# Two MLPs behind LSH attention on one core: order of tasks with a shared port, first norm on VectorE, 45 split tiles on GpSimd

## The chip, the cores and the metric

The kernel runs on one core of one Trainium2 chip. The metric is the device time of one execution in microseconds (us). Five engines work side by side, each in the fixed order of its own instructions: TensorE (PE; its weight loads are listed as PEld), VectorE (DVE), ScalarE (ACT), GpSimd (POOL) and SyncE (SP), which issues the DMAs.

## The reference

```python
batch, n_heads, seq, head_dim = (2, 8, 768, 64)      # attention, 6 hash bits
mask = q_bucket[:, :, :, None] == k_bucket[:, :, None, :]
scores = scale * np.matmul(q, k.transpose(0, 1, 3, 2))
scores = np.where(mask, scores, -1000000000.0)
attn = softmax(scores); x = attn @ v                 # then 1536 tokens x 512
...
xn = x / rms * rms_g                                  # first MLP, d_ff 1536
x = (silu(xn @ w_gate) * (xn @ w_val)) @ w_out
...
h = x @ w_in                                          # second MLP, d_ff 2048
out = elu(h) @ w2_out
```

All values are float32, the weights arrive as float64.

## The kernel before

Every product is made from operands split into a rounded high part and a low rest, so each matmul of the MLPs runs three times (high by high, high by rest, rest by high). The split costs vector work: ScalarE writes the high part, VectorE or GpSimd subtracts it from the value to get the rest.

The attention goes in eight pairs of heads, numbered 0 to 7 here. For a pair, GpSimd writes each head's q and k twice side by side (`twice`, tile `rd`), TensorE transposes it (`prep_T`, `ps_t`), ScalarE and VectorE split it into the operands `tq` and `tk`, and GpSimd copies two of the parts (`tq<-tq`, `tk<-tq`). Hash bits (`ps_b`) and bucket marks (`ps_c`) follow. A pair has six units, each of two blocks of 128 queries: `score` (`ps_s`, the maximum `nm` on VectorE, the exponential on ScalarE), `turn` (three transposed tiles `ps_p` of 128x512 for each unit, each split into `pt`) and `weigh` (`ps_v`). The split of a unit's first tile is done by GpSimd where the table `BYPOOL` names the unit (`phi`, `plo`, from a copy `pf` that ScalarE makes), and by VectorE (L531) elsewhere. `post` divides by the sums of the exponentials (`r`), and `norm` makes the RMS norm of a batch once its four pairs are done: behind pair 3 for the first batch, behind pair 7 for the second. The first norm runs on GpSimd (`newton`, `scale2`, `lo`), the second on VectorE (`scale`).

The weights come in ten groups of matrix parts. `weights` loads a part, ScalarE and VectorE turn its float64 words into float32 (`c1` to `c5`, tile `wf`, L808 to L831), ScalarE writes the high part and GpSimd the rest `wlo` (L856). The first group may be loaded once pair 5 has begun. Then come the MLPs: `hidden` (`ps_h`), `reduce1` (`ps_y`) and `reduce2` (`ps_o`, added to `oa` and stored).

Nothing of this is issued in the order of the text. `Plan` collects tasks with an engine, a duration, what they read and write, and a priority; `Plan.order` then takes, again and again, the task that can start first by these planned durations, and of several the one of lowest priority number. That sequence is each engine's program. The priorities are shifted by the table `OFF`, some 100 numbers. PSUM has four single banks (`bank`) and two double ones (`bank2`); SBUF buffers come from pools of 24 slots, 9 halves and 4 `pt` tiles.

The opening sets constants: on VectorE `wtmp` and `ctmp` (L1085 to L1097) and the projection `pj` (L1114 to L1120), on GpSimd the identity and the fields `bitt` (L1104, L1105).

Of the kernel before, what the change touches and what calls it, by code (L numbers as in the profile page):

```python
# [24 lines left out]
POOL_COPY = 0.82  # L25
# [6 lines left out]
OFF = {'S': [-0.384, -0.596, -1.82, 16.69, -0.785, -0.843, -0.281, -0.374], 'max': [107.091, 86.229, 74.287, 78.306, 4.65, 29.877, -1.002, 35.125], 'exp': [62.941, 112.551, 91.27, 19.546, 123.248, 62.234, 18.002, -5.545], 'T': [0.813, 0.913, 0.365, 0.876, 0.651, 1.113, 1.459, 0.993], 'hi': [19.733, -62.022, -7.959, -72.894, 51.659, 4.387, -74.284, -78.51], 'lo': [37.269, 76.285, 5.085, -95.768, -79.38, 8.342, -31.826, -0.586], 'V': [2.187, 1.975, 1.986, 1.909, 1.876, 2.208, 2.458, 2.096], 'my': [-17.276, -32.546, -64.73, -54.909, -121.029, -34.033, -7.347, -44.516], 'ld': [46.975, -7.846, 214.522, -35.192, 37.247, 221.876, -5.026, -66.279], 'pv': [56.573, -26.315, 46.952, -98.676, 75.721, 70.124, -94.292, -41.006], 'prep': [-0.879, -2.624, -3.589, -0.3, -0.223, -0.105, 0.276, -67.519], 'post': [5.051, 5.005, 2.459, 1.85, 3.722, 8.338, 2.173, 8.692], 'plo': [-134.549, 11.751, -83.073, -44.746, 0.084, -16.015, 72.021, -31.41], 'wc': -3.034, 'ld1': 96.489, 'norm0': -2.712, 'rush': 35.741, 'pstep': 0.316, 'qstep': 0.017, 'norm': 31.762, 'w0': 122.867, 'w0s': 1023313562453027.6}  # L32


class Plan:
# [10 lines left out]
    def __init__(self, caps):  # L46
        self.caps = caps
        self.tasks = []
        self.last_w, self.readers, self.touch, self.duty = {}, {}, {}, {}

    def add(self, eng, us, fn, r=(), w=(), prio=None, lat=0.0, tab=None, duty=1.0):
# [21 lines left out]
        self.duty[i] = duty  # L73
        return i

    def order(self):
# [11 lines left out]
        clock = {}  # L88
        table = None
# [14 lines left out]
        while len(out) < n:  # L104
            best = None
            for eng, lst in ready.items():
                now = clock[eng]
                fits = []
                for i in lst:
                    _, us, fn, deps, bufs, prio, lat, tab = self.tasks[i]  # L110
                    t = max(now, at[i])
                    need = {}
# [42 lines left out]
            clock[eng] = t + us  # L155
            end[i] = t + us + lat
# [22 lines left out]
def kernel(  # L179
# [117 lines left out]
    def prep_v(j, prio):  # L297
# [14 lines left out]
        for a in range(2):  # L312
            plan.add("Pool", 1.4, lambda a=a: hi(a), [("h3", "vn", j)], [(("slot", "vv", j), a, 0)], prio)
# [943 lines left out]
```

## Time and profile before

| | |
|---|---|
| three runs | 861.0, 860.9, 860.76 us, median 860.9 |
| profiled execution | 861.95 us, of which the span of the instructions is 860.2 |
| granted TensorE clock | 0.995 of full speed |
| busy share | PE 97%, DVE 75%, ACT 51%, POOL 32% |
| the chain that ended last | PE 80%, DVE 12%, ACT 4%, POOL 3% of the span |

A share is an average over stages. Pair 0's first score stands at 19.9 us of the span, pair 4's at 142.2, pair 5's at 178.5, pair 6's at 221.8; the last score and the first matmul of the MLPs lie at 280 to 282, and the second batch's norm begins at 309. "Idle" of an engine is time without an instruction in the profile's rows; TensorE's matmuls overlap, and their ends are modelled.

### The profile page before, as it was taken

What the parts mean: (1) busy time and instruction counts of PE and PEld (TensorE: products, weight loads), DVE (VectorE), ACT (ScalarE), POOL (GpSimd) and SP (SyncE); (2) the same over time, 40 slices, a digit from 0 to 9 for tenths busy, and PEclk for the clock granted to TensorE, in tenths of its full rate; (3) what the DMA queues carried; (4) which work ended last, traced back from release to release, by engine and by line L of the source; (5) the groups of instructions that cost most, each with busy time, mean ns of one, the idle gap of its engine ahead of it and who ended that gap; (6) DMA issues with size and microseconds to landing.
All of it is one profiled execution on the core that took longest, in us unless ns stands there. A gap on an engine that the chain in (4) does not pass through costs nothing.

```text
span 860.2 us, 12464 instructions
## 1 busy us (share of the span) xinstructions
PE 836.1 (97%) x4722; PEld 738.2 (86%) x4722; DVE 648.7 (75%) x1020; ACT 440.7 (51%) x831; POOL 279.2 (32%) x295
## 2 busy tenths in 40 slices
PE   7999999998999899999999999999999999999998
PEld 6899999887899799989889898887888888888786
DVE  8999899999999999443265555678856878677754
ACT  3889888898888655332222322245544333332321
POOL 8766576699745322110011110210201111111100
PEclk9999999999999999999999999999999999999999
DMA  5102012240002201211111312204221302001003
GB/s 165 39 19 64 12 38 75 60 146 35 19 2 75 74 1 38 85 31 44 49 50 50 98 50 99 74 1 146 74 74 37 110 25 74 25 25 50 1 12 135
DMA packets 25708, 49.05 MB, mean 57 GB/s; under 512 B 2480, under 2 KB 8880, under 8 KB 25648
## 3 DMA queue, kind: packets, MB, share of 16 engines
q1 hardware_dynamic: 25648, 48.25, 17.2%
q8 instruction: 37, 0.61, 0.3%
q14 instruction: 23, 0.19, 0.1%
HBM read 45.09 MB, written 3.15 MB: 56 GB/s over the span
## 4 chain that ended last, share of the span: by engine, by line
PE 80%; DVE 12%; ACT 4%; POOL 3%; issue 1%; POOLq 0%; DVEq 0%; ACTq 0%
PE ps_h L905 36%; PE ps_o L1044 14%; PE ps_y L990 11%; PE ps_s L474 5%; PE ps_v L566 5%; PE ps_p L519 5%; DVE pt L531 2%; PE ps_t L347 2%; DVE nm L481 2%; PE ps_b L395 1%; ACT p L491 1%; DVE wf L817 1%; DVE wf L824 1%; DVE wf L831 1%; ACT pt L527 1%
## 5 line engine op out<-in xcount | busy, mean ns | idle before, releaser
L856 POOL TENSOR_TENSOR wlo<-wf,whi 128x768 fp32r<-128x768 f32 (+1 forms) x54 | 87.4, 1618 | 444.8 <-ACT whi L852 430.5
L905 PE MATMUL ps_h<-xn,whi 128*128 128x512 f32 (+2 forms) x768 | 190.1, 336 | 2.9 <-DVE pt L531 1.1
L905 PEld LDWEIGHTS ps_h<-xn,whi 128*128 128x128 f32 x768 | 133.6, 189 | 15.6 <-DVE pt L531 1.4
L905 PE MATMUL ps_h<-xn,wlo 128*128 128x256 f32 (+2 forms) x384 | 128.9, 336 | 0.0
L1044 PE MATMUL ps_o<-whi,h 128*128 128x512 f32 (+1 forms) x388 | 118.9, 388 | 0.7 <-DVE oa L1056 0.6
L905 PE MATMUL ps_h<-y,whi 128*128 128x512 f32 x384 | 118.2, 389 | 0.0
L930 ACT ACTIVATE sg<-ps_h 128x512 f32<-128x512 f32 (+1 forms) x87 | 50.6, 583 | 112.6 <-PE ps_h L905 110.4
L852 ACT CAST whi<-wf 128x768 fp32r<-128x768 f32 (+1 forms) x54 | 39.6, 734 | 125.1 <-DVE wf L831 125.0
L566 PE MATMUL ps_v<-pt,vv 128*128 128x256 f32 x576 | 97.9, 296 | 2.2 <-DVE tk L358 1.0
L951 ACT CAST h<-hf 128x512 fp32r<-128x512 f32 (+1 forms) x87 | 51.7, 605 | 88.7 <-DVE hf L936 47.0
L481 DVE TENSOR_REDUCE nm<-ps_s 128x1 f32<-128x768 f32 x96 | 90.8, 946 | 3.1 <-PE ps_s L474 2.4
L990 PE MATMUL ps_y<-h,whi 128*128 128x512 f32 (+1 forms) x312 | 91.3, 373 | 1.3 <-DVE ya L1002 1.3
L491 ACT ACTIVATE p<-ps_s,nm 128x768 f32<-128x768 f32 x96 | 87.2, 909 | 8.3 <-DVE nm L481 7.6
L519 PE MATMUL ps_p<-ident,p 128*128 128x128 f32 x576 | 87.5, 278 | 3.4 <-DVE pt L531 2.6
L474 PE MATMUL ps_s<-tk,tq 128*128 128x384 f32 x384 | 88.2, 351 | 1.0 <-ACT p L491 0.9
L955 DVE TENSOR_TENSOR h<-hf,h 128x512 fp32r<-128x512 f32 (+1 forms) x87 | 69.5, 812 | 25.9 <-ACT h L951 25.1
L1044 PEld LDWEIGHTS ps_o<-whi,h 128*128 128x128 f32 x388 | 72.1, 188 | 16.7 <-DVE oa L1056 2.2
L905 PEld LDWEIGHTS ps_h<-y,whi 128*128 128x128 f32 x384 | 72.1, 188 | 15.0
L936 DVE TENSOR_TENSOR hf<-ps_h,sg 128x512 f32<-128x512 f32 (+1 forms) x39 | 25.2, 647 | 79.0 <-PE ps_h L905 79.0
L566 PEld LDWEIGHTS ps_v<-pt,vv 128*128 128x128 f32 x576 | 78.7, 189 | 5.4 <-DVE pt L531 1.9
L531 DVE TENSOR_TENSOR pt<-ps_p,pt 128x512 fp32r<-128x512 f32 x120 | 80.6, 681 | 3.6 <-ACT pt L527 2.2
L519 PEld LDWEIGHTS ps_p<-ident,p 128*128 128x128 f32 x576 | 67.3, 142 | 12.3 <-DVE pt L531 4.6
(109 smaller groups left out, 1521.3 us busy)
## 6 DMA issues: line engine op xcount, KB each, us to landing
wraw<-in_moe_w_out_dram SPq DMA_DIRECT2D x12, 768.0 KB, 5.1
wraw<-in_moe_w_in_dram SPq DMA_DIRECT2D x8, 768.0 KB, 4.7
wraw<-in_moe_w_out_dram SPq DMA_DIRECT2D x10, 512.0 KB, 4.0
raw<-in_q_dram SPq DMA_DIRECT2D x16, 192.0 KB, 3.1
raw<-in_k_dram SPq DMA_DIRECT2D x16, 192.0 KB, 3.5
vn<-in_v_dram SPq DMA_DIRECT2D x8, 384.0 KB, 3.2
wraw<-in_moe_w_gate_dram SPq DMA_DIRECT2D x4, 768.0 KB, 4.8
wraw<-in_moe_w_val_dram SPq DMA_DIRECT2D x4, 768.0 KB, 4.5
```

Source lines behind the costliest of these rows:

```text
L474: nc.tensor.matmul(st[B_][:, hf, 0:HS], lhsT=tq[:, x, c * 128:(c + 1) * 128], rhs=tk[:, x, hf * HS:(hf + 1) * HS], start=(x == 0), stop=(x ...
L481: nc.vector.tensor_reduce(out=st["nm", u, cc], in_=st[B_][:, :, 0:HS], axis=AX.XY, op=ALU.max, negate=True,)
L491: nc.scalar.activation(out=halves(st["p", u][:, cc]), in_=st.pop(B_)[:, :, 0:HS], func=AF.Exp, bias=st["nm", u, cc], scale=1.0, accum_out= ...
L519: nc.tensor.transpose(out=st[B_][:, o:o + 128], in_=p[:, cc, (2 * n + kt) * 128:(2 * n + kt + 1) * 128], identity=ident,)
L531: nc.vector.tensor_tensor(out=pt[:, 1], in0=st.pop(B_), in1=f(pt[:, 0]), op=ALU.subtract)
L566: nc.tensor.matmul(st[B_][:, 0:256], lhsT=st["vv", j][:, a, 2 * n + kt, :], rhs=pt[:, x, kt * 256:(kt + 1) * 256], start=(n == seq[0] and ...
L856: nc.gpsimd.tensor_tensor(out=l, in0=s["w"], in1=f(h), op=ALU.subtract)
L905: nc.tensor.matmul(ps[:, o:o + ln], lhsT=w[wp][:, kk, ft * 128:(ft + 1) * 128], rhs=t[xp][:, s:s + ln], start=(kk == 0 and n == 0), stop=( ...
L951: nc.scalar.copy(out=st["h", g, blk, ft][:, 0, 0:bw], in_=s["hf"])
L955: nc.vector.tensor_tensor(out=h[:, 1, 0:bw], in0=s["hf"], in1=f(h[:, 0, 0:bw]), op=ALU.subtract)
L990: nc.tensor.matmul(s["ps"][:, 0:bw], lhsT=wo[wp][:, ft, m * 128:(m + 1) * 128], rhs=h[:, xp, 0:bw], start=(ft == 0 and i == 0), stop=(ft = ...
L1044: nc.tensor.matmul(s["ps"], lhsT=h[:, xp, t * 128:(t + 1) * 128], rhs=wo[wp][:, ft, ds], start=(ft == 0 and i == 0), stop=(ft == n - 1 and ...
```

## The change

The planner gets a flag for each task that uses the port which VectorE and GpSimd share: all GpSimd tasks, and those of VectorE that work on SBUF alone. A flagged task is planned to start no sooner than the last flagged one ended. The first norm moves to VectorE, with the code that the second one uses (on ScalarE it issues a load of the activation table ahead of it). GpSimd splits 45 first tiles of units in place of 24: pair by pair 6, 6, 6, 6, 6, 6, 6, 3 in place of 5, 4, 6, 2, 2, 2, 2, 1. `wlo` is written in two halves (twice as many instructions of half the size). In the opening, two of the first four copies `rd` go to VectorE and one to ScalarE, `ctmp` takes three instructions in place of nine, and `bitt` is set by ScalarE. Of the last three sums one uses a single bank. All numbers of `OFF` differ, so the order does everywhere. The names `same_half` and `under` stand for `again` and `across`; their ScalarE forms are not selected.

```diff
-BYPOOL = ([0, 1, 2, 3, 4], [0, 2, 3, 4], [0, 1, 2, 3, 4, 5], [2, 4], [2, 4], [2, 4], [2, 4], [0])
+BYPOOL = ([0, 1, 2, 3, 4, 5], [0, 1, 2, 3, 4, 5], [0, 1, 2, 3, 4, 5], [0, 1, 2, 3, 4, 5], [0, 1, 2, 3, 4, 5], [0, 1, 2, 3, 4, 5], [0, 1, 2, 3, 4, 5], [0, 1, 5])
+FIRST = ('DVE', 'DVE', 'Pool', 'ACT')
+NORM = ('DVE', 'DVE')
...
+        self.port[i] = port or eng == "Pool"
...
+                    if self.port[i]:
+                        t = max(t, port)
...
+            if self.port[i]:
+                port = t + us
...
     def twice(j, a, i, prio):
+        eng = FIRST[2 * a + i] if j == 0 else "Pool"
...
+            cp = {"Pool": nc.gpsimd.tensor_copy, "DVE": nc.vector.tensor_copy, "ACT": nc.scalar.copy}[eng]
...
-        plan.add("Pool", pool(cols), lo, [W_, (H_, part)], [(L_, part)], prio)
+        for x in range(2):
+            plan.add("Pool", pool(cols // 2), lambda x=x: lo(x), [W_, (H_, part)], [(L_, part, x)], prio)
...
+        spare = groups[g][4] and tt >= B * S // 128 - 2 and (tt + ds.start // wd) % 2
+        B_ = ("bank" if spare else "bank2", "o", g, tt, ds.start)
...
-        nc.vector.memset(c[:, 1, 0], 0.0)
-        for i in range(NB):
-            t = ones_of(c[:, 1, 0], i)
-            nc.vector.tensor_scalar(out=t, in0=t, scalar1=-1.0, scalar2=None, op0=ALU.add)
-        nc.vector.tensor_copy(out=c[:, 1, 1], in_=c[:, 1, 0])
-        nc.vector.tensor_scalar(out=c[:, 0], in0=c[:, 1], scalar1=1.0, scalar2=None, op0=ALU.add)
+        nc.vector.tensor_reduce(
+            out=c[:, 1, 0], in_=st["wtmp"].rearrange("o i n -> o n i"), axis=AX.X, op=ALU.add
+        )
...
     def setup_bits():
+        wide = ident.unsqueeze(1).to_broadcast([128, NC, 128])
         for t in bitt:
-            nc.gpsimd.memset(f(t), 0.0)
-            nc.gpsimd.memset(f(t[32:33]), 1.0)
+            v = t.rearrange("p (c n) -> p c n", n=128)
+            nc.scalar.activation(out=v, in_=wide, func=AF.Copy, scale=0.0)
+            nc.scalar.activation(out=v[32:33], in_=wide[32:33], func=AF.Copy, bias=1.0, scale=0.0)
...
-            norm(b, base + UPP + OFF["norm" if j == NPAIR - 1 else "norm0"] - hurry, OFF["qstep"], "Pool" if b + 1 < B else "DVE")
+            norm(b, base + UPP + OFF["norm" if j == NPAIR - 1 else "norm0"] - hurry, OFF["qstep"], NORM[b])
```

VectorE's program in the opening, before the change, from the first write of `ctmp` to the first split of a transposed tile (`pj` is the projection, `tq` the operand made of q):

```order
L1092 MEMSET ctmp 1x64
L1095 TENSOR_SCALAR ctmp<-ctmp 1x32
...
L1096 COPY ctmp<-ctmp 1x64
L1097 TENSOR_SCALAR ctmp<-ctmp 1x128
L1114 CAST pj<-pj_f 128x6
...
L1120 CAST pj<-pj 128x3x18
L358 SCALAR_TENSOR_TENSOR tq<-ps_t,tq 64x384 x2
```

The same place after it:

```order
L1127 TENSOR_REDUCE ctmp<-wtmp 1x64
L1130 TENSOR_SCALAR ctmp<-ctmp 1x128
L1134 TENSOR_SCALAR ctmp<-ctmp 1x128
L343 COPY rd<-raw 128x768 x2
L1155 CAST pj<-pj_f 128x6
...
L1161 CAST pj<-pj 128x3x18
L370 SCALAR_TENSOR_TENSOR tq<-ps_t,tq 64x384 x2
```

Six of the nine `ctmp` instructions are gone, and two copies of the first head's q and k stand between them and the seven instructions of `pj`, which stay ahead of the first split.

GpSimd's program behind pair 3, before the change: the first norm (`z` and `y` are its scale factors, `xT` the tokens, `xn` their rest), with the splits `pt` and copies `tq` that follow:

```order
L697 TENSOR_TENSOR z<-z,y 128x384
L698 TENSOR_SCALAR z<-z 128x384
L701 TENSOR_TENSOR y<-y,z 128x384
L728 TENSOR_TENSOR xT<-xT,y 128x384
L729 TENSOR_TENSOR xT<-xT,gsc 128x384
...
L743 TENSOR_TENSOR xn<-xT,xn 128x384 x2
L728 TENSOR_TENSOR xT<-xT,y 128x384
L729 TENSOR_TENSOR xT<-xT,gsc 128x384
L540 CAST pt<-pf 128x512
L365 CAST tq<-tq 64x384
```

VectorE's program at that place after the change, from the norm's first instructions on, and a later piece of it in the same pair:

```order
L723 TENSOR_TENSOR z<-z,y 128x384
L724 TENSOR_TENSOR z<-z,y 128x384
L725 TENSOR_SCALAR z<-z 128x384
L728 TENSOR_TENSOR y<-y,z 128x384
L558 TENSOR_TENSOR pt<-ps_p,pt 128x512
L454 TENSOR_SCALAR tq<-ps_c 64x384
L748 SCALAR_TENSOR_TENSOR xT<-xT,gsc,y 128x384 x2
...
L427 TENSOR_SCALAR bitt_83<-ps_b 24x384
L770 TENSOR_TENSOR xn<-xT,xn 128x384 x2
L748 SCALAR_TENSOR_TENSOR xT<-xT,gsc,y 128x384 x3
L770 TENSOR_TENSOR xn<-xT,xn 128x384 x3
L611 TENSOR_TENSOR ot<-ps_v,ot 64x256
```

The norm's 24 instructions stand on VectorE now in groups of one to eight between work that reads PSUM; on GpSimd its 32 are gone, and 14 more splits `pt` stand in pairs 4 to 7.

## Rows read from the trace of the kernel before

**Rows 1.** Busy time by stretch: us, then each engine, granted clock, DMA
```profile
0.00:25.00 25.00, 18.77 (x107) 16.47 (x108) 20.95 (x46) 11.20 (x23) 21.32 (x40) 0.93 0.47 143
25.00:142.20 117.20, 115.99 (x856) 110.50 (x855) 108.17 (x176) 102.11 (x218) 76.94 (x97) 1.00 0.12 38
...
178.50:221.80 43.30, 37.14 (x249) 32.03 (x248) 42.60 (x65) 38.28 (x79) 39.13 (x43) 0.98 0.17 54
...
281.80:309.00 27.20, 22.91 (x141) 21.52 (x140) 26.87 (x39) 13.50 (x23) 9.66 (x5) 1.00 0.15 56
309.00:845.00 536.00, 534.10 (x2633) 459.42 (x2632) 350.51 (x537) 190.28 (x314) 73.64 (x48) 1.00 0.17 55
```
**Rows 2.** What TensorE waited for, 178.5 to 309 us
```profile
PE ps_p L519 <- DVE pt L531: 2.4, 3, 1.5
...
PE ps_t L347 <- DVE tq L358: 0.2, 1, 0.2
```
**Rows 3.** Timeline of the opening, in order of time
```profile
1.71 4.64 DVE L1095 TENSOR_SCALAR ctmp<-ctmp 1x32 f32<-1x32 f32 x6
...
2.60 1.21 SPq L1123 DMA_DIRECT2D pj_f<-in_proj_dram  x2
...
9.98 1.00 DVE L358 SCALAR_TENSOR_TENSOR tq<-ps_t,tq 64x384 fp32r<-64x384 f32 x2
...
10.57 2.68 PE L347 MATMUL ps_t<-ident,rd 128*128 128x128 f32 x15 [1.77 <-DVE tq L358]
```
**Rows 4.** DMA issues, first 25 us: KB each, median us to landing
```profile
pj_f<-in_proj_dram SPq DMA_DIRECT2D x2, 1.5 KB, 3.3
```
**Rows 5.** VectorE by line and form, 142.2 to 309 us
```profile
L531 DVE TENSOR_TENSOR pt<-ps_p,pt 128x512 fp32r<-128x512 f32 x72 | 47.9, 678 | 1.0 <-ACT pt L527 0.5
...
L831 DVE SCALAR_TENSOR_TENSOR wf<-wraw,wf 128x768 int32<-128x768 int32 x8 | 10.4, 1300 | 0.0
L811 DVE TENSOR_SCALAR wf<-wf 128x768 f32<-128x768 f32 x8 | 7.9, 992 | 0.1
L824 DVE SCALAR_TENSOR_TENSOR wf<-wraw,wf 128x768 int32<-128x768 int32 x8 | 7.9, 982 | 0.0
L817 DVE TENSOR_SCALAR wf<-wf 128x768 int32<-128x768 int32 x8 | 7.5, 944 | 0.1
```
**Rows 6.** VectorE by line and form, 309 us to the end
```profile
L721 DVE SCALAR_TENSOR_TENSOR xT<-xT,gsc,y 128x384 f32<-128x384 f32 x8 | 4.6, 612 | 0.0
L743 DVE TENSOR_TENSOR xn<-xT,xn 128x384 fp32r<-128x384 f32 x8 | 4.2, 551 | 0.0
L697 DVE TENSOR_TENSOR z<-z,y 128x384 f32<-128x384 f32 x2 | 1.1, 559 | 0.1
```
**Rows 7.** Tile wf on VectorE, 178.5 to 309: ns shortest/median/longest
```profile
L811 DVE TENSOR_SCALAR wf<-wf x8: 547/940/2194, 188.9 to 299.9; 128x768 f32<-128x768 f32 x8
L817 DVE TENSOR_SCALAR wf<-wf x8: 552/620/1643, 191.2 to 302.5; 128x768 int32<-128x768 int32 x8
L824 DVE SCALAR_TENSOR_TENSOR wf<-wraw,wf x8: 895/947/1162, 196.2 to 304.1; 128x768 int32<-128x768 int32 x8
L831 DVE SCALAR_TENSOR_TENSOR wf<-wraw,wf x8: 937/956/2131, 199.6 to 308.5; 128x768 int32<-128x768 int32 x8
```
**Rows 8.** GpSimd by line and form, 142.2 to 309 us
```profile
L543 POOL TENSOR_TENSOR pt<-pf,pt 128x512 fp32r<-128x512 f32 x8 | 12.3, 1549 | 0.3
L743 POOL TENSOR_TENSOR xn<-xT,xn 128x384 fp32r<-128x384 f32 x8 | 8.8, 1100 | 1.2 <-ACT xn L736 1.1
L728 POOL TENSOR_TENSOR xT<-xT,y 128x384 f32<-128x384 f32 x8 | 8.4, 1050 | 0.0
L729 POOL TENSOR_TENSOR xT<-xT,gsc 128x384 f32<-128x384 f32 x8 | 7.4, 926 | 0.6
```
**Rows 9.** ScalarE by line and form, first 330 us
```profile
L688 ACT ACT_TABLE_LOAD x1 | 1.3, 1283 | 0.0
```
**Rows 10.** The page's costliest groups: last sums
```profile
L1044 PE MATMUL ps_o<-whi,h 128*128 128x512 f32 (+1 forms) x388 | 118.9, 388 | 0.7 <-DVE oa L1056 0.6
```

More of the change, by code (lines that the diff above doesn't have):

```diff
@@ L24 @@
 WARM = 16
-POOL_COPY = 0.82
+POOL_COPY = 0.79
+FIRST = ('DVE', 'DVE', 'Pool', 'ACT')
 POOL_HALF = 0.57
@@ L88, in order @@
         clock = {}
+        port = 0.0
         table = None
@@ L609, in post @@
         sums = [(("sum", j), a, c) for a in range(2) for c in range(NC)]
-        plan.add("DVE", 0.1, plus, sums, [R_], prio)
-        plan.add("DVE", 0.17, inv, [], [R_], prio)
+        plan.add("DVE", 0.1, plus, sums, [R_], prio, port=True)
+        plan.add("DVE", 0.17, inv, [], [R_], prio, port=True)
         def widen():
@@ L711, in norm @@
                 lo_eng, 3 * dve(HS) + 0.65 if late else 3 * pool(HS) + 0.75, lambda cs=cs: newton(cs),
-                [], [(Z_, hf), (Y_, hf)], p,
+                [], [(Z_, hf), (Y_, hf)], p, port=True,
             )
@@ L748, in norm @@
                 if late:
-                    plan.add("DVE", dve(HS) + 0.06, scale, [(Y_, hf), "gsc"], [F_], p + step)
+                    plan.add("DVE", dve(HS) + 0.06, scale, [(Y_, hf), "gsc"], [F_], p + step, port=True)
                 else:
@@ L754, in norm @@
                     lo_eng, dve(HS) if late else pool(HS), lo,
-                    [F_, (N_, 0, hf)], [(N_, 1, hf)], p + step,
+                    [F_, (N_, 0, hf)], [(N_, 1, hf)], p + step, port=True,
                 )
@@ L911, in wkeys @@
     def wkeys(g, m):
-        return [(("slot", x, g, m), p) for x in ("whi", "wlo") for p in range(2)]
+        return [(("slot", "whi", g, m), p) for p in range(2)] + [
+            (("slot", "wlo", g, m), p, x) for p in range(2) for x in range(2)
+        ]
     def hidden(g, blk, ft, prio):
@@ L1039, in pe @@
             if "ps" not in s:
-                s["ps"] = bank2("ps_o")[:, 0, 0:wd]
+                s["ps"] = bank("ps_o")[:, 0:wd] if spare else bank2("ps_o")[:, 0, 0:wd]
             wo = st["w", g]["wo"]
@@ L1130 @@
     plan.add("Pool", 1.22, setup, [], ["ident", "pj0"], -30)
-    plan.add("DVE", 0.7, setup_w, [], [("h3", "wtmp")], -30)
-    plan.add("DVE", 6.5, setup_count, [], [("h3", "ctmp")], -30)
+    plan.add("DVE", 0.7, setup_w, [], [("h3", "wtmp")], -30, port=True)
+    plan.add("DVE", 2.2, setup_count, [("h3", "wtmp")], [("h3", "ctmp")], -30, port=True)
     plan.add("Pool", 0.25, setup2, [], ["wsel0"], -29.5)
-    plan.add("Pool", 3.1, setup_bits, [], ["bitt"], -29)
+    plan.add("ACT", 2.9, setup_bits, ["ident"], ["bitt"], -29)
     plan.add("Pool", 0.2, setup3, [], ["ones"], -28)
@@ L1146 @@
         plan.add("PE", 0.218, lambda n=n: warm(n), ["ident"], [("bank", "warm")], 1e6)
-    plan.add("DVE", 2.2, setup_pj, [("pjf", a) for a in range(2)] + ["pj0"], ["pj"], -29)
+    plan.add("DVE", 2.2, setup_pj, [("pjf", a) for a in range(2)] + ["pj0"], ["pj"], -29, port=True)
     wk = []
```

84 lines of the change are left out of this document (55 added, 29 removed).

## Prediction

> **What bounds the kernel now.** I read the busy time by stretch first [rows 1]. From 309 us to 845 us, the MLPs, TensorE is busy 534.1 of 536 us at the full granted clock, so nothing on the other engines can shorten that part: whatever is gained must be gained ahead of 309 us, and is then carried to the end whole, because all work behind it follows in an unbroken row. Ahead of it there are three kinds of stretch. In the first 25 us TensorE idles 6.2 us. From 25 to 142.2 us (most of pairs 0 to 3) it idles 1.2 of 117.2 us while VectorE still has 9 us free: TensorE is the bound. Behind that VectorE is: in pair 5 (178.5 to 221.8) it is busy 42.6 of 43.3 us, GpSimd 39.1, and TensorE idles 6.2; from 281.8 to 309 VectorE is busy 26.9 of 27.2 us and TensorE idles 4.3. The waits of TensorE there say the same: eleven rows, of which the first and the last stand in [rows 2], all name a VectorE instruction, and none GpSimd or a DMA. So the question is what the change does to VectorE's time between about 142 and 309 us, and to the opening.
>
> The second thing to see is how long VectorE's instructions take. Those that read PSUM keep their length: 678 ns in the mean for a tile's split, with GpSimd mostly busy [rows 5]. The four instructions that turn weights into float32 work on SBUF alone, and they do not: the shortest of the first one takes 547 ns, the longest 2194, and the mean is 992 [rows 5, 7]. Means less shortest, 445, 392, 87 and 363 ns, times eight each, give 10.3 us of waiting in 32 instructions, 0.32 us each. I take it that they wait for a GpSimd instruction to end.
>
> The Trainium skill (SBUF — State Buffer, section "Who interferes with whom") says so as a rule: a VectorE instruction with two SBUF inputs, or in a mode that uses both ports, and a GpSimd instruction that reads SBUF exclude each other for a whole instruction. The trace agrees with it in the kinds that are stretched. Its advice is to put such work on the side that is off the critical path, and it thereby speaks against moving the norm; by it alone each moved instruction could wait for a whole GpSimd one, which is the slower rival below.
>
> **The change, part by part.**
>
> *Opening.* The first split of a transposed tile starts at 9.98 us, and TensorE waits 1.77 us for it [rows 3]. What holds VectorE until then is `ctmp`, of which six instructions alone take 4.64 us [rows 3], and behind it `pj`. With `ctmp` short and two copies in its place, VectorE reaches `pj` when its load lands: two issues from 2.60 to 3.81 us, 3.3 us to landing, so near 6.5 to 7.1 [rows 3, 4]. Before, `pj` and what stands ahead of the split went on beside GpSimd's copies; I leave it 1.3 us, which puts the split at about 8.0: a gain of 2.0 us. It could be 1.0 if the copies come late, and at most 4: TensorE's whole idle time of 6.2 us in the first 25 us less the start, which stays. SyncE's queue keeps its order but for `ctmp`'s small load, now ahead of v's. `bitt` on ScalarE costs nothing: that engine is busy 11.2 of the first 25 us [rows 1]; without that cover it would be four instructions ahead of one copy. I take −2.0, bounds −4 to −1.
>
> *Tiles and the norm.* A split costs VectorE 47.9 / 72 = 0.665 us [rows 5]. 14 of the 21 that leave it stand in pairs 4 to 7, where it is the bound: −9.3 us. The norm arrives there: 4.6 for scaling, 4.2 for the rests, three Newton rows of 1.1 and a fourth instruction pair at no more than that, 13.2 us [rows 6]. So +3.9 us in the bound stretch. The other seven tiles, 4.7 us, are freed in pairs 0 to 3, where VectorE is not the bound. They count only as far as later work is drawn forward; between nothing and all of it I take half, −2.4. Sum +1.5, bounds −0.8 to +3.9. The work of ScalarE is the same, since it copies a tile whichever engine splits it.
>
> *GpSimd.* It gets 14 splits in the same stretch at 1.55 us, 21.7 us, and a cast each, and loses 24.6 us of `xn`, `xT` times y and `xT` times g as well as Newton's eight instructions [rows 8]. That is about even, and no wait of TensorE names it: 0.
>
> *Table load.* The norm's code on VectorE brings one load of the activation table on ScalarE, 1.28 us [rows 9], in the pair where the norm runs, and the planner gives it no time. Queued behind it are the root of the norm, then a tile's high part and the next exponentials; a TensorE that waits on VectorE sees little of it. I take +0.3, bounds 0 to 1.3. The Trainium skill (ScalarE: Activation LUTs, section "What ACT_TABLE_LOAD costs") counts 2.66 us for a switch with its drain; the sum would then be at most 1.4 us higher, which the range holds.
>
> *The port.* This is the term that decides. Before: 32 instructions, 10.3 us waited. After: 31 of the weights' instructions ahead of the second norm (by the count of the program) and 24 of the first norm, 55. At the old rate of 0.32 us they wait 17.7 us, +7.4. At the rate of the first weight instruction, 0.45 us, 24.5 us, +14.2. At that of the third, 0.09 us, 4.8 us, −5.5. The third and fourth instruction are of one form, and yet lose 0.7 and 2.9 us in all: where an instruction stands decides, not what it is. The new order places them by a rule that starts none while a GpSimd task is planned to run, so they should lie nearer the low end; but the program is fixed and durations are not, so not at it. I take a third of the old rate, 0.107 us: 5.9 us, −4.4. The halves of `wlo` help: what a VectorE instruction can wait for is shorter.
>
> *Last sums.* TensorE waited 0.6 us for the additions to `oa` in the whole MLP part [rows 10]. A spare bank can save that, but a half sum now stands nearer to the hidden tile that it reads. I take 0, bounds −0.6 to +0.6. The rest of the MLPs' order changes under a TensorE that is full, and costs nothing as long as weights are ready before it asks.
>
> *Sum.* −2.0 + 1.5 + 0 + 0.3 − 4.4 + 0 = −4.6 us. The profiled execution took 861.95 us (span 860.2 and 1.75 around it), so 857.35 for one like it; it lies 1.05 above the median of the runs, which gives 856.3. I say 856.
>
> **Rivals.** *Slower: the norm's instructions collide.* Place: VectorE in pairs 4 and 5, 24 instructions on SBUF alone beside a GpSimd that now has six splits a pair. If the 55 wait at the old rate, the sum is −2.0 + 1.5 + 0.3 + 7.4 = +7.2, or 868; at 0.45 us each, 875. The point from which it decides is 0.19 us an instruction, where the port's term is +0.2 and the sum nil; 0.22 makes the kernel measurably slower. For it: GpSimd is left hardly less busy. (The rule of the Trainium skill's page SBUF — State Buffer, named above, speaks for it too.) Against it: the order was laid so as to avoid this, and the third weight instruction shows that it can be avoided. Chance 0.20.
>
> *No change: the port's rule does not do what it says.* The planned times drift from those on the chip, and the waits settle between 0.16 and 0.22 us an instruction; then the port's term lies between −1.5 and +1.9, and opening, tiles and table cancel: 859.2 to 862.6, in the middle 861. Chance 0.15.
>
> *More is gained.* Waits at the low end (−5.5), all seven early tiles carried (−0.8 in place of +1.5) and the opening at its bound (−4) give −10.0, or 851 with the table. For it: TensorE's idle time ahead of 309 us is 17.9 us in the four stretches shown, and even more could be had. Against: VectorE's own work hardly falls, so these must come together. Chance 0.15.
>
> The forecast, a faster kernel by 2 to 8 us (853 to 859), has the remaining 0.50.
>
> **How the numbers follow.** A difference under 0.2%, 1.7 us, cannot be told from none here. Faster than 859.2 are the forecast and the third rival, 0.65; within, 0.15; slower, 0.20. The range takes in the third rival but for its far end, and the slower one up to waits of 0.27 us, half-way to blind placing's 0.32: 849 to 865. Left out are about 0.05 below and 0.11 above. The likeliest case has its own range, 853 to 859.
>
> **What would show it.** Right: the first split near 8 us; weight and norm instructions on VectorE close to their shortest times (norm 0.55 to 0.61 us, weights 0.55 and 0.9) although GpSimd is busy beside them; the second norm's start moved from 309 to about 304 to 305; TensorE from there on as full as before. Wrong: a mean of 0.8 us or more for the norm's instructions in pair 4 (then the slower rival holds); TensorE waiting for GpSimd's `pt` or `tq`, which it does not do now; a new idle time behind 309 us, where I expect none; or an opening whose first split does not move, since `pj` waits for its load.

## The result and the profile after

The changed kernel takes 866.35 us (median of 4 runs, 864.4 to 866.59) and the kernel before 860.88 us: a ratio of 1.0059 [1.0041, 1.0076]. It is 5.5 us slower; the forecast was 4.9 us faster. The profiled execution after took 866.33 us, span 864.6.

Busy time by stretch, after; columns as in [rows 1]. The third to sixth rows are the pairs 4 to 7, the last is all from pair 4 to the second norm's first matmul:

```profile
0.00:25.00 25.00, 19.01 (x116) 16.42 (x117) 17.32 (x44) 16.27 (x31) 17.33 (x35) 1.00 0.46 143
25.00:143.90 118.90, 117.37 (x872) 112.47 (x870) 105.77 (x173) 102.75 (x222) 86.04 (x109) 1.00 0.12 38
143.90:182.00 38.10, 32.27 (x226) 29.76 (x225) 34.68 (x58) 31.82 (x67) 26.81 (x30) 0.97 0.20 55
182.00:226.20 44.20, 38.09 (x246) 33.38 (x244) 42.45 (x71) 34.87 (x72) 26.38 (x34) 0.94 0.25 87
226.20:262.00 35.80, 32.78 (x234) 29.95 (x232) 33.23 (x51) 28.88 (x60) 24.46 (x26) 1.00 0.04 13
262.00:293.60 31.60, 29.60 (x220) 27.32 (x219) 30.54 (x46) 24.43 (x52) 19.20 (x17) 1.00 0.21 54
...
317.10:849.40 532.30, 532.30 (x2630) 459.25 (x2629) 337.56 (x537) 188.83 (x312) 86.03 (x94) 1.00 0.17 55
143.90:316.20 172.30, 154.69 (x1055) 141.95 (x1054) 160.95 (x254) 135.13 (x272) 107.42 (x115) 0.98 0.18 56
```

The same stretch of the kernel before, from pair 4 to the second norm:

```profile
142.20:308.90 166.70, 155.67 (x1077) 142.52 (x1076) 161.66 (x252) 135.83 (x276) 107.17 (x111) 0.99 0.18 58
```

Read the last two rows first, for they hold the whole case. VectorE is busy 160.95 us where it was busy 161.66, and GpSimd 107.4 where it was 107.2, yet the stretch is 5.6 us longer, with 22 matmuls fewer in it (1055 for 1077; more of them now lie ahead of it). What grew is idle time: VectorE's from 5.0 to 11.4 us, TensorE's from 11.0 to 17.6. With the shift of pair 4's start (142.2 to 143.9) the second norm begins 7.2 us later. Behind it the kernel is faster: from that matmul to the last takes 544.2 us instead of 547.4, and TensorE, which waited there before, is now full in the row 317.1:849.4. The end behind the last matmul is 0.4 us longer. 7.2 − 3.2 + 0.4 gives the 4.4 us by which the spans differ.

What TensorE waited for from pair 4 to the second norm, after (columns: in all, times, longest):

```profile
PE ps_v L593 <- DVE pt L558: 4.2, 6, 1.5
PE ps_p L546 <- ACT pf L563: 3.6, 2, 3.4
PE ps_p L546 <- DVE ot L611: 2.8, 2, 2.5
PE ps_c L443 <- DVE pt L558: 1.4, 1, 1.4
PE ps_p L546 <- ACT tk L452: 1.4, 2, 0.7
PE ps_s L501 <- ACT p L518: 1.3, 2, 1.2
```

Before, every row of this view named VectorE, those of [rows 2] among them. VectorE's sum is much the same; ScalarE is new, with 6.3 us in these rows. The longest wait, in the order of time:

```profile
169.94 1.28 ACT L715 ACT_TABLE_LOAD   x1
171.24 0.52 ACT L717 ACTIVATE y<-z 128x384 f32<-128x384 f32 x1
171.79 0.52 ACT L718 ACTIVATE y<-y 128x384 f32<-128x384 f32 x1
172.34 0.59 ACT L554 CAST pt<-ps_p 128x512 fp32r<-128x512 f32 x1
172.82 0.53 ACT L717 ACTIVATE y<-z 128x384 f32<-128x384 f32 x1
173.38 0.52 ACT L718 ACTIVATE y<-y 128x384 f32<-128x384 f32 x1
173.93 0.49 ACT L452 ACTIVATE tq<-ps_c 64x384 fp32r<-64x384 f32 x1
174.44 0.59 ACT L563 COPY pf<-ps_p 128x512 f32<-128x512 f32 x1
...
175.08 0.65 PE L546 MATMUL ps_p<-ident,p 128*128 128x128 f32 x4 [3.39 <-ACT pf L563]
```

TensorE needs a bank that `pf`, a split tile's copy, is to empty. ScalarE works its queue in order, and ahead of that copy stand the table load and both halves of the norm's roots.

TensorE's clock fell as well. It has two levels, 2.4 and 1.2 GHz, and in two places of this stretch it stood at the lower one for some 3 us, so that the granted clock of 4 us is 0.57:

```profile
180.00:184.00 4.00, 3.73 (x16) 3.33 (x16) 3.85 (x8) 2.59 (x6) 1.55 (x2) 0.57 1.01 297
...
214.00:218.00 4.00, 4.00 (x21) 4.00 (x21) 4.00 (x7) 3.46 (x7) 2.42 (x4) 0.57 0.00 0
```

In the 10 us ahead of these places TensorE had been busy 4.5 and 5.9 us. The profiled execution of the kernel before has one such place, at 220 us, and experiment 4 shows what it costs there: 0.9 us. By the rows above it could be 0.43 of 4 us, 1.7 us, at most (an estimate).

VectorE by line and form in the stretch, after, which answers to [rows 5] and, for the norm, to [rows 6]:

```profile
L558 DVE TENSOR_TENSOR pt<-ps_p,pt 128x512 fp32r<-128x512 f32 x54 | 36.2, 681 | 3.4 <-ACT pt L554 2.9
L851 DVE SCALAR_TENSOR_TENSOR wf<-wraw,wf 128x768 int32<-128x768 int32 x7 | 6.9, 990 | 0.0
L838 DVE TENSOR_SCALAR wf<-wf 128x768 f32<-128x768 f32 x8 | 6.7, 843 | 0.1
L858 DVE SCALAR_TENSOR_TENSOR wf<-wraw,wf 128x768 int32<-128x768 int32 x7 | 6.5, 933 | 0.0
L844 DVE TENSOR_SCALAR wf<-wf 128x768 int32<-128x768 int32 x8 | 6.5, 823 | 0.0
L748 DVE SCALAR_TENSOR_TENSOR xT<-xT,gsc,y 128x384 f32<-128x384 f32 x8 | 6.0, 784 | 0.0
L770 DVE TENSOR_TENSOR xn<-xT,xn 128x384 fp32r<-128x384 f32 x8 | 5.6, 732 | 0.0
```

The tiles freed VectorE of 47.9 − 36.2 = 11.7 us. That is 18 tiles, not the 14 of the pairs 4 to 7, since the stretch begins and ends at other places of the work than before. VectorE's idle time just before its splits went from 1.0 to 3.4 us, 2.9 of it until ScalarE had written the high part. The weights' instructions, measured against the shortest of [rows 7], waited 2.4 + 2.2 + 0.7 + 0 = 5.2 us (10.3 before). The norm's took 16.9 us in all with its eight Newton instructions, some 4 us above the lengths of [rows 6]. That is 9.2 us in 54 instructions, 0.17 us each: half the rate of before, and not the third that I had put in.

The opening, after, which answers to [rows 3]:

```profile
3.27 1.25 DVE L343 COPY rd<-raw 128x768 f32<-128x768 f32 x2 [0.32 <-DMA raw<-in_q_dram]
...
6.21 0.17 DVE L1155 CAST pj<-pj_f 128x6 fp32r<-128x6 f32 x1 [1.69 <-DMA pj_f<-in_proj_dram]
...
7.12 1.00 DVE L370 SCALAR_TENSOR_TENSOR tq<-ps_t,tq 64x384 fp32r<-64x384 f32 x2
...
13.14 0.44 PE L422 MATMUL ps_b<-tk,pj 128*128 128x384 f32 x1 [1.25 <-POOL tk L387]
```

The first split stands at 7.12 us (9.98 before), 0.9 us earlier than forecast. `pj` now waits for its load, and TensorE then waits 1.25 us for a copy of GpSimd, so that the first score is only 1.4 us earlier, at 18.5 us.

### The profile page after: what moved, and what is told of

Read it like the earlier page. It is cut to its first block, busy times and chain, and to the rows that moved or that the text cites. A ratio compares the mean times of both kernels' runs of the same rounds, so it can differ in the third digit from the quotient of the medians.

```text
span 864.6 us, 12523 instructions
## 1 busy us (share of the span) xinstructions
PE 835.5 (97%) x4722; PEld 739.8 (86%) x4722; DVE 629.8 (73%) x1019; ACT 444.2 (51%) x837; POOL 296.8 (34%) x352
## 4 chain that ended last, share of the span: by engine, by line
PE 82%; DVE 9%; ACT 6%; issue 2%; DMA 1%; POOL 1%; SPq 0%; DVEq 0%; ACTq 0%; POOLq 0%
PE ps_h L937 38%; PE ps_o L1079 15%; PE ps_y L1024 11%; PE ps_s L501 5%; PE ps_v L593 5%; PE ps_p L546 4%; DVE pt L558 2%; DVE nm L508 2%; ACT p L518 2%; PE ps_t L359 2%; ACT pt L554 1%; PE ps_b L422 1%; DVE xT L748 1%; ACT pf L563 1%; DVE tq L454 1%
## 5 line engine op out<-in xcount | busy, mean ns | idle before, releaser
L887 POOL TENSOR_TENSOR wlo<-wf,whi 128x384 fp32r<-128x384 f32 (+1 forms) x108 | 102.1, 966 | 429.7 <-ACT whi L879 366.5
L593 PE MATMUL ps_v<-pt,vv 128*128 128x256 f32 x576 | 95.9, 298 | 5.1 <-DVE pt L558 4.4
L518 ACT ACTIVATE p<-ps_s,nm 128x768 f32<-128x768 f32 x96 | 87.5, 911 | 11.9 <-DVE nm L508 11.1
L546 PE MATMUL ps_p<-ident,p 128*128 128x128 f32 x576 | 83.8, 276 | 9.0 <-ACT pf L563 3.6
L989 DVE TENSOR_TENSOR h<-hf,h 128x512 fp32r<-128x512 f32 (+1 forms) x87 | 64.5, 757 | 22.1 <-ACT h L985 21.5
L546 PEld LDWEIGHTS ps_p<-ident,p 128*128 128x128 f32 x576 | 66.6, 141 | 16.1 <-ACT pf L563 4.7
L937 PEld LDWEIGHTS ps_h<-xn,wlo 128*128 128x128 f32 x384 | 72.7, 189 | 5.7
```

What stands on the lines that cost most here:

```text
L518: nc.scalar.activation(out=halves(st["p", u][:, cc]), in_=st.pop(B_)[:, :, 0:HS], func=AF.Exp, bias=st["nm", u, cc], scale=1.0, accum_out= ...
L546: nc.tensor.transpose(out=st[B_][:, o:o + 128], in_=p[:, cc, (2 * n + kt) * 128:(2 * n + kt + 1) * 128], identity=ident,)
L593: nc.tensor.matmul(st[B_][:, 0:256], lhsT=st["vv", j][:, a, 2 * n + kt, :], rhs=pt[:, x, kt * 256:(kt + 1) * 256], start=(n == seq[0] and ...
L887: nc.gpsimd.tensor_tensor(out=l[z], in0=s["w"][z], in1=f(h[z]), op=ALU.subtract)
L937: nc.tensor.matmul(ps[:, o:o + ln], lhsT=w[wp][:, kk, ft * 128:(ft + 1) * 128], rhs=t[xp][:, s:s + ln], start=(kk == 0 and n == 0), stop=( ...
L989: nc.vector.tensor_tensor(out=h[:, 1, 0:bw], in0=s["hf"], in1=f(h[:, 0, 0:bw]), op=ALU.subtract)
```

## The experiments

My theory after the result: the parts cost and free VectorE what I said, but VectorE's freed time is not given back as time, since the new order makes engines wait. The rivals: the norm on VectorE is dearer than forecast; the further splits are the cost; the port is. No expectation names TensorE's clock, so its part is read from the rows afterwards. Each run was timed beside the kernel before on the same chip; "stretch" below is pair 4's start to the second norm's first matmul.

**1. No table load for the first norm.** The changed kernel with

```
-                if late:
+                if late and b + 1 == B:
                     nc.scalar.preload_act_table_set("natural_log_exp_and_others")
```

> The kernel after, without the one load of the activation table that the first norm brings on ScalarE (1.28 us); nothing else moves. Theory NORM (the first norm on VectorE is what costs the time: its instructions and its table load hold attention work that stands behind them on VectorE and ScalarE, which shows as TensorE's 3.4 us wait for ScalarE's pf at 175 us and 2.5 us for VectorE's ot at 208 us): 1.0 to 2.0 us less, 864.3 to 865.4. Theory ORDER (the whole order got worse, wherever the norm runs): within 0.5 us of 866.35. Theory PORT (waits for the shared port): no change either.

864.9 us, 1.0042 [1.0030, 1.0054]: by the medians the load costs 1.45 us, as theory NORM has it, but the interval overlaps that of the changed kernel (1.0041 to 1.0076). The Trainium skill (ScalarE: Activation LUTs, section "What ACT_TABLE_LOAD costs") counts 2.66 us with the drain for a switch to a different set of functions. This load names the set that ScalarE has in use already; its row has 1.28 us and the time 1.45, below the page's figure for a switch. I had 0.3. The experiments on the changed kernel below start from this one.

**2. The first norm on GpSimd in the new order.** Every instruction of the norm at its place, but issued to GpSimd (L723 to L728, L748 as two multiplications, L770).

> The kernel after, with the first norm's arithmetic issued on GpSimd again (no table load either), at the same places of the program, so that nothing else moves. NORM: VectorE is 13 us lighter in pairs 4 and 5, the two TensorE waits of 3.4 and 2.5 us go, 858 to 862. ORDER: 865 to 869, since the order stays and GpSimd gets 32 us more. PORT: a few us less at most, 862 to 866, as the 24 instructions waited about 4 us in all.

876.34 us, 1.0177 [1.0164, 1.0190], above all three ranges. Busy time of pair 5:

```profile
184.20:237.20 53.00, 41.60 (x246) 37.45 (x244) 33.90 (x56) 34.90 (x72) 44.99 (x56) 0.83 0.26 88
```

VectorE is busy 33.9 of 53 us here, GpSimd 45. Beside 45 splits, GpSimd is the worse place for the norm in this order. How much of the time is GpSimd's work and how much the clock that falls with TensorE's waits (0.83 in this row, 0.94 in the changed kernel's pair 5) isn't separated.

**3. The kernel before, its first norm on VectorE.** The norm's instructions in the old order, on the other engine:

```
-            eng = nc.vector if late else nc.gpsimd
+            eng = nc.vector
...
-                    plan.add("Pool", 2 * pool(HS), scale2, [(Y_, hf), "gsc"], [F_], p + step)
+                    plan.add("Pool", 2 * pool(HS), scale, [(Y_, hf), "gsc"], [F_], p + step)
```

> The kernel before, with the first norm's arithmetic issued on VectorE at the places where GpSimd had it; nothing else moves. NORM: 13 us of VectorE's time arrive in a stretch that it bounds, 867 to 874. ORDER: 859 to 863. PORT: waits of 24 instructions at 0.17 to 0.32 us each, 4 to 8 us, on top of NORM's.

871.71 us, 1.0109 [1.0092, 1.0127]: +10.7 us. The stretch:

```profile
142.10:319.00 176.90, 158.44 (x1077) 143.80 (x1076) 171.55 (x276) 136.26 (x276) 75.31 (x79) 0.98 0.17 55
```

VectorE got 9.9 us more work and the stretch 10.2 us longer, 1.03 for each microsecond. Not all of that is VectorE's work: two of the six executions, with a mean granted clock of 0.998, took 868.0 us, and the other four, at 0.992 to 0.995, 871.6 to 872.4; the profiled one is of these and has two falls of the clock in the stretch, at 207 and 220 us. By the two at 0.998 the norm costs 7.0 us, 0.7 for each. The norm's 24 instructions waited 0.1 us in all for the port here, where GpSimd is busy 75 us and not 107.

**4. The new opening in the old order.** `FIRST`, `ctmp` from one reduction, `bitt` on ScalarE; nothing else.

> The kernel before, with the new opening alone (two of the first copies on VectorE, one on ScalarE, ctmp in three instructions, bitt on ScalarE), in the same order. If the opening's gain of 1.4 us at the first score is carried: 859.0 to 859.8. If it is lost behind: 860.5 to 861.2.

859.93 us beside 860.98, 0.9989 [0.9980, 0.9998]: −1.05 us. In its profile the second norm begins 2.0 us earlier. Of these, 1.1 us are gained in the opening and carried unchanged to 220 us. The other 0.9 us are the clock's: in the kernel before it falls there, and in this execution it does not (1.00 from 219 to 223 us). The same matmuls, first of the kernel before, then of this run:

```profile
220.18 1.97 PE L519 MATMUL ps_p<-ident,p 128*128 128x128 f32 x8
221.80 1.63 PE L474 MATMUL ps_s<-tk,tq 128*128 128x384 f32 x4
```

```profile
219.10 1.25 PE L520 MATMUL ps_p<-ident,p 128*128 128x128 f32 x8
220.10 0.95 PE L475 MATMUL ps_s<-tk,tq 128*128 128x384 f32 x4
```

TensorE had been busy 8.5 of the 10 us ahead of them in both.

**5. The low parts of weights in halves, in the old order.**

```
-            nc.gpsimd.tensor_tensor(out=l, in0=s["w"], in1=f(h), op=ALU.subtract)
+            for x in range(2):
...
+                nc.gpsimd.tensor_tensor(out=l[z], in0=s["w"][z], in1=f(h[z]), op=ALU.subtract)
```

> The kernel before, order untouched; only GpSimd's subtraction that makes the low part of a weight tile (L856) is issued as two halves. Two things are tested. First, the stalls of TensorE at the layers' joints (0.52, 1.10 and 0.76 us at 552, 599 and 815 us before, none of them in the changed kernel): if the halves removed them, the part behind the second norm's first matmul falls from 547.4 to about 545.0 us. If something else in the new order did, it stays at 547.4. Second, the port: VectorE's 31 weight instructions of 142 to 309 us each waited 0.33 us before. If an instruction that waits does so for the end of the GpSimd instruction under way, halves shorten that, to about 0.17 us (minus 5 us of VectorE's time) or at the most to nothing. Theory (halves remove the joints' stalls and half of the waits): 854 to 858 us. Rival (the halves do neither): 861 us. Only the joints: 858.5 us.

859.66 us beside 861.7, 0.9976 [0.9967, 0.9984]. TensorE's waits behind the second norm, first of the kernel before, then of this one:

```profile
PE ps_y L990 <- DVE ya L1002: 1.3, 2, 0.9
PE ps_o L1044 <- DVE oa L1056: 0.6, 1, 0.6
```

```profile
PE ps_o L1049 <- DVE oa L1061: 0.6, 1, 0.6
```

Two of the three stalls at the joints go, and that part takes 545.9 instead of 547.4 us. Waits for the port hardly change: VectorE's 41 SBUF-only instructions of the stretch, each less the shortest of its form, waited 11.3 us (12.5 before), so the second half of that theory fell. The Trainium skill (SBUF — State Buffer, section "Who interferes with whom") has the two engines exclude each other for a whole instruction. The trace agrees in which kinds are stretched, but halving one kind of GpSimd's instructions took only a tenth of the waits away.

**6. The low parts of the 21 new splits back on VectorE**, in the new order:

```
-            nc.gpsimd.tensor_tensor(out=st[T_][:, 1], in0=st["pf", u], in1=f(st[T_][:, 0]), op=ALU.subtract)
+            eng = nc.gpsimd if u % NC in OLD[j] else nc.vector
+            eng.tensor_tensor(out=st[T_][:, 1], in0=st["pf", u], in1=f(st[T_][:, 0]), op=ALU.subtract)
```

> The changed kernel without the table load for the first norm (864.9 us), in the same order; the low parts of the 21 score tiles that were not split before go from GpSimd back to VectorE (their copies out of PSUM stay on ScalarE and their high parts on GpSimd). 14 of them lie in the pairs 4 to 7; at about 0.6 us each VectorE's work from the start of pair 4 to the second norm rises from 160.5 to about 169 us and GpSimd's falls from 107 to about 95. The theory that the splits make the new idle time of VectorE (11 us of that stretch, 5 before, since it waits for a chain over ScalarE and GpSimd): the idle time falls back to about 5 us and the kernel takes 866 to 868 us. The rival that the order leaves VectorE idle whatever GpSimd does: the idle time stays near 11 us and the kernel takes 872 to 875 us.

868.34 us, 1.0082 [1.0068, 1.0096], +3.4 us on the 864.9. VectorE's busy time rose only from 160.5 to 164.2 us, since its waits for the port, counted as in experiment 5, fell from 11.1 to 6.1 us (the norm's own from 4.0 to 1.8); its idle time went from 9.6 to 7.8. The time agrees with the splits' theory at its edge, the idle time with neither. What it does show: a low part given to GpSimd frees VectorE of some 0.6 us and takes about half of it back at the port.

**7. The norm on GpSimd, with an order worked out for it.** `NORM = ('Pool', 'DVE')` in the changed kernel; without the norm on VectorE there is no table load for it.

> The changed kernel with the first norm back on GpSimd and the order worked out anew for that (the 45 splits, the port in the rules and the table of numbers stay; no table load). With the order made for VectorE's norm the same thing took 876.3 us. If that was a matter of the order (tasks queued on GpSimd behind a norm that the plan had put elsewhere), a plan that knows it takes 856 to 863 us. If 45 splits and the norm are too much for GpSimd (133 us of work in 172, nearly all of the pairs 4 and 5), no order helps and it takes 868 to 877 us; pairs 4 and 5 are then each several us longer than the changed kernel's 38.1 and 44.2.

893.1 us, 1.0365 [1.0351, 1.0379], above both ranges. Pair 5:

```profile
179.40:244.00 64.60, 41.44 (x227) 32.88 (x225) 38.84 (x61) 36.34 (x74) 53.19 (x59) 0.82 0.15 56
```

GpSimd is busy 53 of 64.6 us and still idles 11, so it is not GpSimd's capacity alone. The table of numbers was made for another plan, and the clock is 0.82 in this row. The run doesn't separate the three.

**8. Three parts of the change in the old order**: opening, halves, spare banks.

> The kernel before in its own order, with three parts of the change that need no other order: the new opening, the low parts of weights in halves, and the spare banks for the last sums. It has neither the 21 further splits, nor the norm on VectorE, nor the port in the planner's rules. If the parts add up: minus 1.05 us for the opening (measured), minus 2.4 us at the joints, 0 to minus 5 us of waits for the port, 0 to minus 0.4 us at the end: 852 to 857.5 us, below both kernels. If the halves do nothing: 859.9 us.

857.78 us beside 861.7, 0.9963 [0.9951, 0.9976], just above the range. This one beats both kernels. Opening and halves alone would make −1.05 − 2.04 = −3.1 us; measured are −3.9, whose interval holds −3.1 too. From the second norm's first matmul on it is 0.3 us shorter than experiment 5: at the last sums a weight load of TensorE no longer waits 0.28 us for `oa`.

**9. The norm's instructions apart.** In the new order, each of L748 and L770 is queued behind another instruction of VectorE:

```
+            if i in self.spread:
+                late.append(i)
+                continue
...
+            while late and n >= 1:
+                k = late.pop(0)
+                self.tasks[k][2]()
```

> The changed kernel without the table load for the first norm (864.9 us), every engine's work as there; only the first norm's scalings, copies and low parts (L748, L770) are queued so that VectorE never has two of them in a row: each stands behind another instruction of VectorE. The theory that the norm costs by standing in runs on an engine that works its queue in order (2.5 us of TensorE's wait behind the run that ends at 208 us, 2.1 us at 178 us): TensorE's waits in the pairs 4 and 5 fall by 2 to 4 us, and the kernel takes 861 to 863 us. The rival that only the sum of VectorE's work counts: VectorE's idle time stays near 9.6 us and the time within 1 us of 864.9 us.

865.75 us, 1.0053 [1.0040, 1.0065]: no gain on 864.9. TensorE's waits in the stretch:

```profile
PE ps_v L607 <- DVE pt L572: 5.4, 6, 1.5
PE ps_p L560 <- ACT pf L577: 2.5, 2, 2.3
PE ps_p L560 <- ACT tk L466: 2.5, 2, 1.6
```

The wait behind `ot`, 2.4 us in experiment 1, is gone and comes back elsewhere: TensorE idles 16.3 us in the stretch, 15.2 in experiment 1. That theory of mine falls.

**10. One planner constant changed**: `HOP` 0.17 for 0.16.

> The changed kernel without the table load for the first norm (864.9 us); the planner counts 0.17 instead of 0.16 us from one engine to the next where no other figure is listed. Nothing that an engine computes changes, but the order does, from the first pair on, since the table of numbers was made for the other plan. It shows how much of a time belongs to one particular order. If the rules and the splits decide, the time stays within 2 us of 864.9 us. If the particular order decides, it moves by 4 us or more, more likely up: 868 to 885 us.

883.54 us, 1.0250 [1.0236, 1.0264]: 18.6 us more, with the same work on every engine. One particular order carries more time than all parts of the change together. The clock's share in it is 7 us at most (an estimate: its mean over the profiled execution is 0.988, in experiment 1 0.996; the shortfall times the span is 10.6 and 3.4 us).

**11. Fewer late splits, order worked out anew.** `BYPOOL` with only [2, 4], [2, 4], [2, 4], [0] for the pairs 4 to 7.

> The changed kernel without the table load for the first norm (864.9 us); in the pairs 4 to 7 only the 7 tiles of the kernel before are split (21 in the changed kernel), in the pairs 0 to 3 all 24, and the order is worked out anew by the same rules and numbers. VectorE gets 14 whole tiles back at 0.665 us, 9.3 us of work from pair 4 to the second norm, and GpSimd loses some 25 us there. If the splits were worth what VectorE's work says: 872 to 875 us. If they cost nearly as much in waits for the port and for the chain over ScalarE and GpSimd as they freed (moving the low parts alone gave VectorE 8.7 us of work and took 5 us of such waits from it): 866 to 870 us. Up to 5 us either way can come from the new order itself, which the run with the other hop shows.

888.99 us, 1.0322 [1.0306, 1.0339], above both ranges. After the run above this says nothing of the splits: a new order can cost that much by itself.

So the last three runs keep their order and take work away.

**12. Work taken from VectorE in the old order.**

```
+            w = 32 if brief(u, n) else 512
...
+                        rhs=pt[:, 1, 0:32].unsqueeze(1).to_broadcast([128, 8, 32])
+                        if x and brief(u, n) else pt[:, x, kt * 256:(kt + 1) * 256],
```

> The kernel before in its own order, with nothing moved; for the 21 tiles that the change splits, VectorE works out only 32 of the 512 columns of the low part (L531), and TensorE multiplies those 32 again and again in their place: the low part of these tiles is left out, every matmul and every dependence stays. VectorE thus gets rid of about 0.53 us for each, 7.5 us for the 14 tiles of the pairs 4 to 7 and 3.7 us for the 7 of the pairs 0 to 3, and no other engine gets anything for it. The theory of the prediction (the stretch of 142 to 309 us lasts as long as VectorE's work): the second norm comes 7.5 us earlier and the kernel takes 853 to 854 us. The rival (VectorE's freed time turns into waits of VectorE, since TensorE and ScalarE hold each other in a fixed order): less than half of it, 857 to 860 us. Both expect nothing from the 7 early tiles.

856.67 us beside 861.92, 0.9942 [0.9928, 0.9957]. The cut tiles on VectorE, and the stretch:

```profile
L536 DVE TENSOR_TENSOR pt<-ps_p,pt 128x32 fp32r<-128x32 f32 x21 | 3.9, 184 | 0.5 <-ACT pt L531 0.3
```

```profile
142.00:303.50 161.50, 152.49 (x1077) 141.81 (x1076) 153.93 (x251) 134.99 (x276) 106.31 (x111) 1.00 0.19 60
```

VectorE has 7.7 us less work, and the stretch is 5.2 us shorter: 0.67 of it comes back, between the theory and the rival. The fall of the clock at 220 us isn't there in this execution; without the 0.9 us that it costs in the kernel before, 4.3 us or 0.56 come back. Pair 4 starts at 142.0 us (142.2 before) and the first score at 20.5 (19.9), so the 7 early tiles bring 0.8 us of the 3.7 that they free.

**13. The same in the old order with the norm on VectorE.**

> The same cut (32 of 512 columns of the low parts of the 21 tiles, the rest left out) in the kernel before with its first norm on VectorE (871.7 us), in the same order. If VectorE's work sets the stretch: 7.5 us less, 864 us. If freed time turns into waits: 867 to 870 us. Together with the run before it this shows whether work taken from VectorE is worth more when VectorE is the more loaded.

868.29 us, 1.0070 [1.0049, 1.0090], its executions between 864.9 and 871.1. In the profile VectorE's work falls by 6.0 us (171.5 to 165.5) and the stretch by 4.8 (176.9 to 172.1), or 0.8. One of the two falls of the clock in experiment 3's stretch is gone here; by the medians 3.4 us come back, or 0.57.

**14. The norm's work taken away in the new order.** Newton's steps and the scalings on 32 columns:

```
+                    if b + 1 < B:
+                        xs = (*xs[:2], slice(xs[2].start, xs[2].start + 32))
```

> The changed kernel without the table load for the first norm (864.9 us), in the same order; of the first norm VectorE's Newton steps and scalings (L723 to L728, L748, 16 instructions) do only the first 32 columns of each half, so that the most of this norm's arithmetic is left out and every dependence stays. VectorE loses some 8 to 10 us of work between 171 and 212 us, waits for the port among them. In the kernel before, the norm's move put 16.9 us on VectorE and cost 10.7 us, 0.63 for one. If it costs as much in the new order: 5 to 6 us less, 859 to 860 us. If the norm's instructions lie in VectorE's waits there: within 1.5 us of 864.9 us.

862.03 us, 1.0002 [0.9993, 1.0011]: 2.9 us less than 864.9, between the two. The stretch, first of experiment 1, then of this run:

```profile
143.80:313.90 170.10, 154.95 (x1055) 141.69 (x1054) 160.52 (x255) 133.74 (x271) 107.39 (x115) 0.98 0.17 57
```

```profile
144.20:312.40 168.20, 155.11 (x1054) 142.02 (x1053) 153.18 (x254) 132.97 (x271) 106.50 (x115) 0.98 0.18 57
```

VectorE lost 7.3 us of work and the stretch 1.9: 0.26. The row of experiment 1 is of the fastest of its five executions; by the medians 2.9 us come back, 0.39. Set this run's row beside the one of experiment 12: VectorE 153.2 and 153.9 us, GpSimd 106.5 and 106.3, but 168.2 us against 161.5. With the same loads of these two the new order takes 6.7 us longer. The granted clock differs: 1.00 there, and 0.98 here, with two falls, at 178 and 219 us. At 0.9 to 1.7 us each they make 1.8 to 3.4 of the 6.7 us (an estimate).

## Why the prediction was wrong

**The step that failed** is that VectorE bounds the stretch from 142 to 309 us, used as if the stretch lasted as long as VectorE's work in any order. The sum that I made of that work came out: +3.9 for the tiles and the norm and −4.4 for the port, or −0.5; measured 161.66 to 160.95, −0.7. In part that was luck: the port missed by 3.3 us, and the stretch lost 18 splits in place of 14, and two weight instructions. But the stretch grew by 5.6 us. In the old order a microsecond of VectorE's work that is added costs 0.7 to 1.03 us, and one that is taken away gives 0.56 to 0.67 (0.57 to 0.8 with the norm on VectorE). In the new order, where TensorE also waits for ScalarE, it gives 0.26 to 0.39; there it was work of the norm and not of the splits, so this is not like for like. VectorE was 97% busy before and is 93% busy now; a step that converts work into time has to be priced for the order in which the work will stand, and that price was not in my sum or my bounds. Nor did they have TensorE's waits for ScalarE (6.3 us in the rows above, none before) or its clock, which falls in one place more than before: 0.9 to 1.7 us by the estimate above.

**Opening.** Mechanism right; −2.0 forecast, −1.05 measured alone, at the near bound. In the changed kernel a wait for GpSimd's copy took part of it, which I had not named. The clock has a part here too: with the same new opening the first score stands at 18.7 us in experiment 4 and at 19.3 in experiment 8, where the clock falls at 14 us.

**Tiles and the norm.** The norm's +13.2 us measured +10.7 in the old order, 7.0 in the executions at the higher clock. The 14 tiles' −9.3: a cut of VectorE's work of 7.7 us in the old order brought 5.2. The early seven's −2.4 was too much: TensorE is as full from 25 us to pair 4 as before (117.37 of 118.9 us), and in experiment 12 the 3.7 us that these tiles freed brought 0.8. "Half of it" was a guess where my own reading had TensorE as the bound.

**GpSimd.** Right that it is about even (107.2 and 107.4 us) and that TensorE doesn't name it there. But its added splits make the norm wait at the port: some 4 us here, 1.8 without their low parts (experiment 6), 0.1 with the emptier GpSimd of experiment 3.

**Table load.** 0.3 forecast, 1.45 measured by medians whose intervals overlap, just above the bound of 1.3: TensorE sat at that moment behind ScalarE and not behind VectorE.

**The port.** Forecast −4.4 at 0.107 us, measured 0.17 us and −1.1. I had put the point from which the slower rival decides at 0.19. So the kernel became slower without that rival's condition: its sign was right, its mechanism not. By its rate, 0.17 belongs to the rival of no change, at 861 us. The halves of `wlo`, counted as a help, took 1.2 of 12.5 us of such waits away in experiment 5.

**Last sums and what lies behind 309 us.** That nothing on the other engines can shorten that part was wrong by 3.2 us: TensorE's three stalls at the layers' joints and a fourth at the last sums are gone. The halves of `wlo` take two of them (1.5 us), the spare banks 0.3 us at the end, and the one at 814 us (0.6) went with the new order; the remaining 0.8 us aren't accounted for. The end grew by 0.4 us.

**The account.** Opening −1.05, norm +10.7, table +1.45, joints −3.2 and the end +0.4 make +8.3 us; measured is +5.5. The 21 splits, the port's rule and the new order are thus worth −2.8 together, where tiles and port were forecast at −16.1 (−9.3, −2.4 and −4.4). With the norm at 7.0 us, by the executions at the higher clock, the parts make +4.6, and the rest +0.9. Experiment 12 puts the tiles alone, without GpSimd's part, at −5.25 in the old order (0.9 of it the clock's in the profiled execution). These are differences of runs in two orders, so the account is a reading and not a proof. Of the 6.7 us that the new order costs at the same loads, the clock explains 1.8 to 3.4 by the estimate. The cause of the rest is open: the run that spread the norm's instructions didn't find it, and neither the new splits without the port's rule nor the old splits with it were measured.

## What to carry to other kernels

A bound engine's work is time only while the order lets it stay busy: price a re-made order by what it makes the other engines wait for, in their queues too, and ask for each removed microsecond who is idle next. Look at TensorE's granted clock in both traces before a difference is put down to the order: a fall of it comes and goes between executions of one order, and cost 0.9 us here. Before crediting a new order's parts, issue each of them in the old order; here three small parts, so issued, beat both kernels (857.78 us). And an order fitted to one plan is brittle: 0.01 us in a planner's constant cost 18.6 us.

## What was not expected of the hardware

- A table load for functions that ScalarE was already using cost 1.28 us in its row and, by the medians, 1.45 us of the kernel's time.
- TensorE's clock fell to the lower level at 220 us in one execution and not in another with the same instructions there: eight matmuls took 1.97 us in the first and 1.25 in the second. In experiment 3 the executions lie at 868.0 us (mean clock 0.998) and near 872 (0.992 to 0.995).
- VectorE's subtraction out of PSUM takes 184 ns for 32 columns and 681 to 683 for 512, so about 0.15 us of it doesn't depend on the columns.
- The norm's 24 instructions on VectorE waited 0.1 us for the port beside a GpSimd that was busy 75 of 177 us, and some 4 us, in another order, beside one busy 107 of 172: far more than GpSimd's load grew. In the pairs 4 and 5 alone, where the norm stands, GpSimd was busy 33 of 90 us and 53 of 82.
